# Convolution of large token groups in 32x32 tiles of the matmul array

## The chip, the cores and the metric

The kernel runs on one core of a Trainium2 chip. The metric is the time of one execution on the device in microseconds (us), taken as the median of several runs. A hardware profile of one execution gives the traces that are read here. The engines of the core are TensorE (PE, its weight loads are listed as PEld), VectorE (DVE), ScalarE (ACT), GpSimd (POOL) and SyncE (SP, which here only issues DMAs). SBUF is the on-chip memory of 128 partitions, PSUM the small memory that PE writes into, and DRAM the memory outside.

## The reference

The input x holds 8 sequences of 4160 tokens with 192 channels, in float32. The channels are 8 heads of 24. Two steps are computed.

```python
# step 1: causal convolution over 7 tokens, one softmaxed filter a head
w = softmax(weight)                                  # (8, 7)
y[b, s, h*24:(h+1)*24] = sum_k w[h, k] * x_pad[b, s + k, h*24:(h+1)*24]
# step 2: channel mix
xk = mu_k * y + (1 - mu_k) * y_prev                  # y_prev: the token before
xr = mu_r * y + (1 - mu_r) * y_prev
k  = maximum(xk @ w_k, 0)                            # 192 -> 1024
v  = (k * k) @ w_v                                   # 1024 -> 192
out = v / (1 + exp(-(xr @ w_r)))                     # w_r: 192 -> 192
```

The output is 8 x 4160 x 192 in float32. The kernel works in bf16 with sums in float32.

## The kernel before, in words

**Pairs, steps, slots, bundles.** The 8 sequences go in four pairs. Both sequences of a pair are worked on together: their transposed y, `yT`, has 128 partitions, 64 channels of the one and 64 of the other, in three chunks. A pair is cut into steps of 512 tokens (some are 256), 34 steps in all. A step is cut into slots; a slot is one PSUM tile of k, 128 hidden channels by 512 tokens by two sequences (`k_mm`, L537, then relu on ACT, `k_relu`, L549, then the square on DVE, `k_square`, L563). Four slots make a bundle, and there are 65 bundles. The order of all engines is written out by hand: `bundle_rest` (L861) emits a bundle's work, and tables (`early`, `mix_a`, `mix_b`, `mix_c`, `late`, `xt`, `rq`, `rs`, `vq`) say which piece of other work goes to which place of which bundle.

**What a bundle holds.** In order on PE: three blocks of k (18 matmuls of 512 columns), the gate product r (`r`, L594, 12 matmuls), the first half of v (`v_rows`, L625, 32 matmuls), the fourth block of k, the convolution units of this bundle if there are any, and the second half of v. `v_out` (L641) multiplies v by the gate on DVE and SP stores it. All PSUM tiles come from one ring of four tiles of two banks; a tile is reused when the engine that reads it is done. `diff` (L480), `scale` (L511) and `add_y` (L517) make xk and xr from `yT` on DVE; the `diff` of a step stands two bundles ahead of the step's first bundle, in `mix_c`.

**Convolution.** A filter over 7 tokens is a banded matrix `toe` over tokens, so the convolution is a matmul that contracts tokens. The tokens of a pair are cut into groups. The first four groups are small and are done in other ways at the start (`conv_t`, L371, which yields y transposed, with 128x32 tiles; `conv_mm`, L351). The other 14 groups, g4 to g17, are large: three of 10 and one of 8 for each of the last three pairs, with "10" meaning two halves of ten blocks of 56 tokens (1120 tokens). Block rows are 64 tokens of which 6 are the halo and 56 give results, so one matmul uses a 64x64 tile of the array. `conv_tiles` (L302) does one unit: two heads, 8 matmuls, two row tiles by two column tiles, one PSUM tile. `conv_tiles_out` (L319) casts it into the tile `y` on ACT, in one piece or in two where the heads straddle a chunk of 64 channels. A group has four units, two in each of two bundles that lie two apart.

**The way of a group.** For a group needed by the step whose first bundle is fb, the units stand in bundles fb - 9 and fb - 7. `x_tile` (L103) takes a tile from a pool of three, sets one element on DVE (L109), and `load_x` (L116) loads x with a cast to bf16 from POOL's queue (L136), 8 to 15 bundles before fb; the element on DVE holds the load back until DVE has come that far. After the last unit, `y_write` (L424) writes y to DRAM by four DMAs of SP's queue; two bundles later (one for the first two of these groups) `y_read` (L432) reads it back by one transposing DMA into `yT`. `y` has two tiles.

**Names that the prediction uses.** k_sb is relu's output, r_sb the gate, o_sb the output tile (three buffers), xb the x tile, ps_c, ps_k, ps_r, ps_v, ps_t the PSUM tiles of convolution, k, r, v and transposing convolution.

Of the kernel before, what the change touches and what calls it, by code (L numbers as in the profile page):

```python
# [7 lines left out]
FP32 = mybir.dt.float32  # L8
BF16 = mybir.dt.bfloat16
# [5 lines left out]
def kernel(  # L15
# [11 lines left out]
    nc = tc.nc  # L27

    B, S, D = x.shape
# [8 lines left out]
    BLK = 120  # L38
    GB = 10
    HB = 56  # L40
    NROW = -(-S // (2 * HB)) * 2 * HB
    BANK = 512
    STEP = 512
# [45 lines left out]
    for p in range(NPAIR):  # L89
        base = 0  # L90
        for nb, s, on_pe in (
            ((3, 0, True), (4, 1, True), (4, 2, True), (5, 3, True), (10, 4, False), (10, 6, False))
            if p == 0
            else ((10, 0, False), (10, 2, False), (10, 4, False), (8, 6, False))
        ):
            groups.append((p, base, nb, first_bundle[first_step[p] + s], on_pe))
            base += nb * (BLK if on_pe else 2 * HB)
        assert S <= base <= NROW


    xbs = {}

    def x_tile(g):  # L103
        p, base, nb, _, on_pe = groups[g]
        xb = three.tile([P, GB, 2, D], BF16, tag="xb", name="xb")
        xbs[g] = xb
        if g > 4:

            nc.vector.memset(xb[0:1, 0, 0, 0:2], 0.0)  # L109
        if base == 0:  # L110
            nc.gpsimd.memset(xb[0:32, 0, :, :], 0.0)  # L111
        if not on_pe and base + 2 * nb * HB > S:
            n0 = nb - (base + 2 * nb * HB - S) // HB - 1
            nc.gpsimd.memset(xb[Q:P, n0:nb, :, :], 0.0)

    def load_x(g):  # L116
        p, base, nb, _, on_pe = groups[g]
        xb = xbs[g]
        if on_pe:
            parts, step, rows = ((0, base),), BLK, P  # L120
        else:
            parts, step, rows = ((0, base), (Q, base + nb * HB)), HB, Q
        for s in range(2):
            b = 2 * p + s
            for q0, start in parts:
                lo, hi = 0, nb
                t0 = start - HALO
                if t0 < 0:
# [94 lines left out]
    def softmax():  # L223
        nc.vector.tensor_reduce(out=w_max, in_=w_raw, axis=mybir.AxisListType.X, op=ALU.max, negate=True)
        nc.scalar.activation(out=w_exp, in_=w_raw, func=AF.Exp, bias=w_max, accum_out=w_sum)
        nc.scalar.preload_act_table(AF.Sigmoid)
        xbs[0] = three.tile([P, GB, 2, D], BF16, tag="xb", name="xb")
        for c in range(NC):
            cs = slice(c * Q, (c + 1) * Q)
            nc.scalar.copy(out=xbs[0][:, : groups[0][2], :, cs], in_=x_f32[:, :, :, cs])  # L230
# [78 lines left out]

    def conv_tiles_out(g, c):  # L310

        m = groups[g][2] // 2
        ps = conv_ps.pop((g, c))
        y = ys[g]
        c0, c1 = 2 * c * G, 2 * (c + 1) * G
        cuts = [c0] + [a for a in range(Q, D, Q) if c0 < a < c1] + [c1]
        for a, b in zip(cuts, cuts[1:]):
            d = a // Q * 2 * Q + a % Q
            nc.scalar.copy(  # L319
                out=bass.AP(  # L320
                    tensor=y.tensor,
                    offset=y.offset + d,
                    ap=[y.ap[0], [m * 2 * D, 2], [2 * D, m], [Q, 2], [1, b - a]],
                ),
                in_=bass.AP(
                    tensor=ps.tensor,
                    offset=ps.offset + a - c0,
                    ap=[ps.ap[0], [BANK, 2], [4 * G, m], [2 * G, 2], [1, b - a]],
                ),
            )  # L330

    def conv_units(g):

# [76 lines left out]
    def new_yT(p):  # L410
        yTs[p] = two.tile([P, 3, -(-(YC + S) // 16) * 16], BF16, tag="yT", name="yT")
        y_drams[p] = dram.tile([NROW, 2 * D], BF16, tag=f"y{p % 2}", name="y_dram")
        nc.vector.memset(yTs[p][:, :, 0:YC], 0.0)


    def y_write(g):
        p, base, nb, _, _ = groups[g]
        if base == 0:
            new_yT(p)
        m = nb // 2  # L420
        for j in range(2):
            for i in range(2):
                r0 = base + (i * nb + j * m) * HB
                nc.sync.dma_start(  # L424
                    out=y_drams[p][r0 : r0 + m * HB, :].rearrange("(n t) c -> t n c", t=HB),
                    in_=ys[g][j * Q : j * Q + HB, i * m : (i + 1) * m, :],
                )

    def y_read(g):
        p, base, nb, _, _ = groups[g]  # L430
        r0, r1 = base, min(base + 2 * nb * HB, S)
        nc.sync.dma_start_transpose(  # L432
            out=yTs[p][:, :, YC + r0 : YC + r1], in_=y_drams[p][r0:r1, :]
        )
# [244 lines left out]
    def at(table, b, fn, *a):  # L679
        table.setdefault(b, []).append((fn, a))  # L680
# [7 lines left out]
    for g, (p, base, nb, fb, on_pe) in enumerate(groups):  # L688
        if g < 3:
            continue  # L690
        if p == 0:
            xs = {3: [1, 1], 4: [2, 2, 3, 3], 5: [4, 4, 5, 5]}[g]
        else:
            xs = [fb - 9] * 2 + [fb - 7] * 2
        for i, b in enumerate(xs):
            xt.setdefault(b, []).append((g, i))
        if not on_pe:
            at(late, xs[-1], y_write, g)

            at(mix_c if g == 4 else late, xs[-1] + (1 if g < 6 else 2), y_read, g)  # L700
        if g > 4:

# [53 lines left out]
    def prologue():  # L756
# [13 lines left out]
        nc.vector.memset(zeros, 0.0)  # L770
        nc.vector.memset(w_nrm, 0.0)
        nc.vector.memset(ones6, 1.0)
        x_tile(1)
        load_x(1)
        masks_tap()
# [85 lines left out]
    def bundle_rest(b, ns):  # L861
# [131 lines left out]
```

## Time and profile before

| what | value |
|---|---|
| median of the runs | 414.11 us (413.73 to 414.35, 3 runs) |
| span of the profiled execution | 412.2 us |
| lies around the span, by the median | 1.9 us |
| PE busy | 403.7 us |
| DVE busy | 370.5 us |
| ACT busy | 353.2 us |
| POOL busy | 64.1 us |
| matmuls of the large groups (L302) | 448, busy 16.6 us |
| casts of the large groups (L319) | 84, busy 50.7 us |

The span runs from the first to the last instruction in the profiled execution; that execution has no time of its own beside it, and the median of the runs stands for it. Busy is the time in which an engine works on at least one instruction. Matmuls overlap, so the busy time of a group of them is less than their number times the length of one. "The chain" is the work that ended last, followed back from the end: at each step to what released it. A row such as `204.98 1.88 ACT L319 CAST ... x3` gives start, length, engine, line, operation, shapes and how many were merged; brackets at its end give idle time before it and what ended that. SPq rows are DMA issues in SP's queue, their length is that of the issue and not of the transfer. In a table of windows a row gives the window, its length, the busy time of PE and of PEld with the number of instructions in it, the granted clock, the share of DMA time and GB/s.

### The profile page before, as it was taken

How to read it: one execution, taken by the hardware profiler on the slowest of the kernel's cores; microseconds unless marked ns; L12 is line 12 of the kernel's file. 1: busy time of each engine (PE TensorE's matmuls, PEld its weight loads, DVE VectorE, ACT ScalarE, POOL GpSimd, SP SyncE). 2: the span in 40 equal slices, each digit the busy share in tenths (PEclk: the TensorE clock that was granted, in tenths of full speed). 3: DMA queues.
4: the chain of work that ended last, by engine and by line, in shares of the span. 5: the costliest groups of instructions: out<-in, count | busy, mean ns of one | idle time of the engine just before them, and what ended most of it. 6: DMA issues, size and time to landing. Idle time of an engine off the chain costs nothing.

```text
span 412.2 us, 16799 instructions
## 1 busy us (share of the span) xinstructions
PE 403.7 (98%) x7349; PEld 301.7 (73%) x7350; DVE 370.5 (90%) x672; ACT 353.2 (86%) x426; POOL 64.1 (16%) x100
## 2 busy tenths in 40 slices
PE   7899999999999999999999999999999999999996
PEld 5567767767867777776777777777777777777795
DVE  5999799999999998999999999999989898999973
ACT  6899978889988888988888899888889888787781
POOL 8622023022040201104040110304000000000000
PEclk9999999999999999999999999999999999999999
DMA  9999989959978894998769697897863926321223
GB/s 141 192 200 194 191 200 190 253 133 194 198 110 211 151 214 118 200 218 113 198 121 229 156 196 182 111 226 130 188 163 100 184 82 175 107 67 53 80 80 115
DMA packets 137241, 65.58 MB, mean 159 GB/s; under 512 B 87356, under 2 KB 137168, under 8 KB 137168
## 3 DMA queue, kind: packets, MB, share of 16 engines
q1 hardware_dynamic: 95840, 48.42, 44.9%
q0 software_dynamic: 40528, 15.53, 33.0%
q8 instruction: 57, 0.93, 0.9%
q10 hardware_dynamic: 800, 0.57, 0.4%
q14 instruction: 16, 0.13, 0.1%
HBM read 31.62 MB, written 37.09 MB: 167 GB/s over the span
## 4 chain that ended last, share of the span: by engine, by line
PE 88%; DMA 4%; DVE 3%; ACT 2%; issue 1%; POOL 1%; SPq 0%; POOLq 0%
PE ps_v L625 39%; PE ps_k L537 37%; PE ps_r L594 7%; PE ps_c L302 3%; DMA yT<-y_dram 2%; DMA wk<-in_moe_w_k_dram 2%; DVE k L563 1%; PE ps_v L577 1%; DMA y_dram<-y 1%; ACT k_sb L549 1%; ACT y L319 0%; DVE d L480 0%; POOL xb L136 0%; DVE xr L511 0%; SPq L424 0%
## 5 line engine op out<-in xcount | busy, mean ns | idle before, releaser
L549 ACT ACTIVATE k_sb<-ps_k 128x1024 bf16<-128x1024 f32 x260 | 253.1, 1037 | 36.1 <-PE ps_k L537 35.2
L563 DVE TENSOR_TENSOR k<-k_sb 128x1024 bf16<-128x1024 bf16 x260 | 172.6, 685 | 28.3 <-ACT k_sb L549 27.9
L537 PE MATMUL ps_k<-xk,wk 64*128 64x512 bf16 (+1 forms) x1632 | 191.0, 367 | 1.2 <-DMA wk<-in_moe_w_k_dram 0.7
L625 PE MATMUL ps_v<-wv,k 64*128 64x192 bf16 x4032 | 188.2, 243 | 0.2 <-DVE k L563 0.2
L625 PEld LDWEIGHTS <-k 64*128 64x128 bf16 x4032 | 167.7, 94 | 13.6 <-issue 4.0
L537 PEld LDWEIGHTS <-wk 64*128 64x128 bf16 x1632 | 79.9, 94 | 59.6 <-DMA wk<-in_moe_w_k_dram 0.9
L136 POOL DMA_DIRECT2D xb<-in_x_dram x62 | 45.1, 738 | 171.2 <-issue 81.8
L641 DVE TENSOR_TENSOR o_sb<-ps_v,r_sb 128x768 f32<-128x768 f32 x64 | 60.8, 951 | 2.6 <-issue 2.4
L605 ACT ACTIVATE r_sb<-ps_r 128x768 bf16<-128x768 f32 x65 | 53.3, 821 | 10.6 <-PE ps_v L625 9.9
L319 ACT CAST y<-ps_c 128x960 bf16<-128x960 f32 (+5 forms) x84 | 50.7, 685 | 0.0
L594 PEld LDWEIGHTS <-xr 64*128 64x128 bf16 x780 | 34.5, 94 | 15.2 <-issue 1.0
L594 PE MATMUL ps_r<-wr,xr 64*128 64x192 bf16 x780 | 43.1, 243 | 0.5 <-DVE o_sb L641 0.5
L511 DVE TENSOR_SCALAR xr<-d,mu 128x512 bf16<-128x512 bf16 (+1 forms) x102 | 35.1, 348 | 0.0
L480 DVE TENSOR_TENSOR d<-yT 128x1536 bf16<-128x1536 bf16 (+4 forms) x36 | 31.3, 870 | 2.0 <-ACT yT L381 1.1
L511 DVE TENSOR_SCALAR xk<-d,mu 128x512 bf16<-128x512 bf16 (+1 forms) x99 | 32.0, 352 | 0.1
L517 DVE TENSOR_TENSOR xr<-xr,yT 128x1536 bf16<-128x1536 bf16 (+1 forms) x33 | 31.0, 938 | 1.1
L517 DVE TENSOR_TENSOR xk<-xk,yT 128x1536 bf16<-128x1536 bf16 (+3 forms) x33 | 30.4, 921 | 0.1
L302 PEld LDWEIGHTS <-toe 64*64 64x64 bf16 x448 | 9.6, 106 | 11.7 <-issue 10.7
L302 PE MATMUL ps_c<-xb,toe 64*64 64x240 bf16 (+1 forms) x448 | 16.6, 265 | 0.2 <-ACT k_sb L549 0.2
L464 POOL COPY y_tail<-yT 128x195 bf16<-128x195 bf16 x4 | 3.2, 796 | 64.9 <-DMA yT<-y_dram 64.8
L111 POOL MEMSET xb<- 32x384 bf16 x3 | 1.2, 407 | 45.2 <-DVE xb L109 39.2
L371 PEld LDWEIGHTS <-xb 128*32 128x32 bf16 (+3 forms) x264 | 5.3, 119 | 1.9 <-ACT xb L230 1.1
(57 smaller groups left out, 63.0 us busy)
## 6 DMA issues: line engine op xcount, KB each, us to landing
out_dram<-o_sb SPq DMA_DIRECT2D x128, 192.0 KB
xb<-in_x_dram POOLq DMA_DIRECT2D x40, 240.0 KB, 8.2
y_dram<-y SPq DMA_DIRECT2D x44, 210.0 KB
y_dram<-y SPq DMA_DIRECT2D x12, 168.0 KB
xb<-in_x_dram POOLq DMA_DIRECT2D x10, 192.0 KB, 5.5
xb<-in_x_dram POOLq DMA_DIRECT2D x6, 216.0 KB, 4.9
xb<-in_x_dram POOLq DMA_DIRECT2D x6, 144.0 KB, 5.3
wk<-in_moe_w_k_dram POOLq DMA_DIRECT2D x4, 192.0 KB, 7.1
```

Source lines behind the costliest of these rows:

```text
L136: nc.gpsimd.dma_start(out=xb[q0 : q0 + rows, lo:hi, s, :], in_=bass.AP(tensor=x.tensor, offset=x.offset + (b * S + t0 + lo * step) * D, ap ...
L302: nc.tensor.matmul(out=banks[j * Q : (j + 1) * Q, i, :, :, k * G : (k + 1) * G], lhsT=toe[q, h, q], rhs=xbs[g][q, j * m : (j + 1) * m, :, ...
L319: nc.scalar.copy(out=bass.AP(tensor=y.tensor, offset=y.offset + d, ap=[y.ap[0], [m * 2 * D, 2], [2 * D, m], [Q, 2], [1, b - a]],), in_=bas ...
L511: nc.vector.tensor_scalar(out=t[:, c, :L], in0=diffs[s][:, c, :L], scalar1=mu[:, i, c : c + 1], scalar2=None, op0=ALU.mult)
L517: nc.vector.tensor_tensor(out=o, in0=o, in1=y_of(s, sl, 0), op=ALU.add)
L537: nc.tensor.matmul(out=ps[:, i, f * L : (f + 1) * L], lhsT=wk[r, c, fs], rhs=xk[r, c, :L], start=c == 0 and f == 0, stop=c == NC - 1 and f ...
L549: nc.scalar.activation(out=k_sb, in_=ps.rearrange("p a b -> p (a b)"), func=AF.Relu)
L563: nc.vector.tensor_tensor(out=o, in0=i, in1=i, op=ALU.mult)
L594: nc.tensor.matmul(out=ps[:, i, k * D : (k + 1) * D], lhsT=xr[q, c, ts], rhs=wr[q, c, :], start=c == 0, stop=c == NC - 1,)
L605: nc.scalar.activation(out=r_sbs[s, j], in_=r_ps.pop((s, j))[:, :, 0 : 2 * D], func=AF.Sigmoid)
L625: nc.tensor.matmul(out=v_ps[s, j][:, bank, k * D : (k + 1) * D], lhsT=k2s[s][q, f, t * P : (t + 1) * P], rhs=wv[q, f, :], start=half == 0 ...
L641: nc.vector.tensor_tensor(out=o_sb.rearrange("p (b t) d -> p b (t d)", b=2), in0=v_ps.pop((s, j)), in1=r_sbs.pop((s, j)), op=ALU.mult,)
```

## The change

From the middle of the second pair on, groups have a third kind, marked `None` where `on_pe` was True or False: 80 blocks of 26 tokens, 2080 tokens a group. There are five of them, g8 to g12, in place of the ten groups g8 to g17 of before; g4 to g7 stay. The first, in the second pair, begins at token 2080 and overlaps the group before it, of which only the rows up to there are read back.

A block row is now 32 tokens, 6 of halo and 26 of results; four row tiles by four column tiles of 32x32 hold 16 matmuls. `conv_sparse` does one unit: two heads, 32 matmuls of 240 columns into two PSUM tiles, each row tile into a bank of its own. Then each of the two tiles is cast into its own `y` tile by the pieces of before. A group has four units, one in each of four bundles: fb - 11, -9, -7 and -5 (15, 16, 17 and 19 for the first one).

A group's `y` are both tiles of the pool. They are written by eight DMAs of 26 partitions by 10 blocks after the last unit, and read back in two halves, at the ends of bundles fb - 4 and fb - 1. The x tiles now come from two tiles of 20 blocks; the small groups 0 to 3 share one, 4 and 5 the next, 6 and 7 the next. A large group is loaded in two halves, one a sequence, 18 and 14 bundles ahead of fb (15 and 13 for the first), each held back by an element that DVE sets (`tie_x` for the second).

```diff
@@ groups
-            else ((10, 0, False), (10, 2, False), (10, 4, False), (8, 6, False))
+            else ((10, 0, False), (10, 2, False), (TG, 4, None))
+            if p == 1
+            else ((TG, 0, None), (TG, 4, None))
...
+            if on_pe is None:
+                base = min(base, S - nb * 4 * TB)
@@ x_tile
-        xb = three.tile([P, GB, 2, D], BF16, tag="xb", name="xb")
+        if g in (0, 4, 6) or g in sparse:
+            whole = two.tile([P, TG, 2, D], BF16, tag="xb", name="xb")
+            room[:] = [whole, 0]
+        xb = room[0][:, room[1] : room[1] + nb, :, :]
@@ load_x
+        elif g in sparse:
+            parts, step, rows = [(32 * i, base + i * nb * TB) for i in range(4)], TB, 32
...
-        for s in range(2):
+        for s in batches:
@@ new
+    def conv_sparse(g, c):
+        nb = groups[g][2]
+        m = nb // 4
+        if c == 0:
+            ys[g] = [two.tile([P, GB, 2 * D], BF16, tag="y", name="y") for _ in range(2)]
+        tiles = [ring.tile([P, 2, BANK], FP32, tag="k", name="ps_c") for _ in range(2)]
+        xb = xbs[g].rearrange("p (m j) s c -> p j m s c", j=4)
+        for k in range(2):
+            h = 2 * c + k
+            for i in range(4):
+                q = slice(32 * i, 32 * i + 32)
+                banks = tiles[i // 2][:, i % 2, 0 : m * 4 * G].rearrange("p (m s c) -> p m s c", m=m, s=2)
+                for j in range(4):
+                    nc.tensor.matmul(
+                        out=banks[32 * j : 32 * j + 32, :, :, k * G : (k + 1) * G],
+                        lhsT=toe[q, h, q],
+                        rhs=xb[q, j, :, :, h * G : (h + 1) * G],
+                        start=True,
+                        stop=True,
+                    )
+        for y, ps in zip(ys[g], tiles):
+            cast_tiles(y, ps, m, c)
@@ y_write
+        if g in sparse:
+            m = nb // 4
+            for half in range(2):
+                for j in range(4):
+                    nc.sync.dma_start(
+                        out=bass.AP(
+                            tensor=y_drams[p].tensor,
+                            offset=y_drams[p].offset + (base + (2 * half * nb + j) * TB) * 2 * D,
+                            ap=[[2 * D, TB], [4 * TB * 2 * D, 2 * m], [1, 2 * D]],
+                        ),
+                        in_=ys[g][half][32 * j : 32 * j + TB, :, :],
+                    )
+            return
@@ tables
+        elif p == 1:
+            xs = [fb - 9, fb - 8, fb - 7, fb - 5]
         else:
-            xs = [fb - 9] * 2 + [fb - 7] * 2
+            xs = [fb - 11, fb - 9, fb - 7, fb - 5]
...
+        if g in sparse:
+            at(late, fb - 4, y_read, g, slice(0, 1), 2)
+            at(late, fb - 1, y_read, g, slice(1, 2), 2)
+            b = fb - 18 if p > 1 else fb - 15
+            at(early, b, x_tile, g)
+            at(early, b, load_x, g, (0,))
+            b = fb - 14 if p > 1 else fb - 13
+            at(early, b, tie_x, g, 1)
+            at(early, b, load_x, g, (1,))
+            continue
@@ bundle_rest
         for u in units:
-            conv_tiles(*u)
-            conv_tiles_out(*u)
+            if u[0] in sparse:
+                conv_sparse(*u)
+            else:
+                conv_tiles(*u)
+                conv_tiles_out(*u)
```

TG is 20 and TB 26. `cast_tiles` is the body of the former `conv_tiles_out` with the tiles as arguments.

More of the change, by code (lines that the diff above doesn't have):

```diff
@@ L40 @@
     HB = 56
+    TB = 26
+    TG = 20
     NROW = -(-S // (2 * HB)) * 2 * HB
@@ L93, with tie_x @@
             if p == 0
-            else ((10, 0, False), (10, 2, False), (10, 4, False), (8, 6, False))
-        ):
+            else ((10, 0, False), (10, 2, False), (TG, 4, None))
+            if p == 1
+            else ((TG, 0, None), (TG, 4, None))
+        ):
+            if on_pe is None:
+                base = min(base, S - nb * 4 * TB)
             groups.append((p, base, nb, first_bundle[first_step[p] + s], on_pe))
-            base += nb * (BLK if on_pe else 2 * HB)
+            base += nb * (4 * TB if on_pe is None else BLK if on_pe else 2 * HB)
         assert S <= base <= NROW
-    xbs = {}
+    sparse = {g for g, grp in enumerate(groups) if grp[4] is None}
+    ends = [nxt[1] if nxt[0] == grp[0] else S for grp, nxt in zip(groups, groups[1:] + [(NPAIR,)])]
+    xbs, room = {}, []
+    def tie_x(g, s):
+        nc.vector.memset(xbs[g][0:1, 1, s, 0:2], 0.0)
     def x_tile(g):
         p, base, nb, _, on_pe = groups[g]
-        xb = three.tile([P, GB, 2, D], BF16, tag="xb", name="xb")
+        if g in (0, 4, 6) or g in sparse:
+            whole = two.tile([P, TG, 2, D], BF16, tag="xb", name="xb")
+            room[:] = [whole, 0]
+        xb = room[0][:, room[1] : room[1] + nb, :, :]
+        room[1] += nb
         xbs[g] = xb
@@ L109, in x_tile, with load_x @@
             nc.vector.memset(xb[0:1, 0, 0, 0:2], 0.0)
-        if base == 0:
+        if base == 0 and g > 0:
             nc.gpsimd.memset(xb[0:32, 0, :, :], 0.0)
-        if not on_pe and base + 2 * nb * HB > S:
+        if on_pe is False and base + 2 * nb * HB > S:
             n0 = nb - (base + 2 * nb * HB - S) // HB - 1
             nc.gpsimd.memset(xb[Q:P, n0:nb, :, :], 0.0)
-    def load_x(g):
+    def load_x(g, batches=range(2)):
         p, base, nb, _, on_pe = groups[g]
@@ L226, in softmax @@
         nc.scalar.preload_act_table(AF.Sigmoid)
-        xbs[0] = three.tile([P, GB, 2, D], BF16, tag="xb", name="xb")
         for c in range(NC):
             cs = slice(c * Q, (c + 1) * Q)
-            nc.scalar.copy(out=xbs[0][:, : groups[0][2], :, cs], in_=x_f32[:, :, :, cs])
+            nc.scalar.copy(out=xbs[0][:, :, :, cs], in_=x_f32[:, :, :, cs])
         nc.vector.reciprocal(out=w_sum, in_=w_sum)
@@ L310, in conv_tiles_out, with cast_tiles @@
     def conv_tiles_out(g, c):
-        m = groups[g][2] // 2
-        ps = conv_ps.pop((g, c))
-        y = ys[g]
+        cast_tiles(ys[g], conv_ps.pop((g, c)), groups[g][2] // 2, c)
+    def cast_tiles(y, ps, m, c):
         c0, c1 = 2 * c * G, 2 * (c + 1) * G
@@ L427, in y_write, with y_read @@
                 )
-    def y_read(g):
-        p, base, nb, _, _ = groups[g]
-        r0, r1 = base, min(base + 2 * nb * HB, S)
+    def y_read(g, part=slice(0, 1), of=1):
+        p, base = groups[g][:2]
+        n = (ends[g] - base) // of
+        r0, r1 = base + part.start * n, base + part.stop * n
         nc.sync.dma_start_transpose(
@@ L692 @@
             xs = {3: [1, 1], 4: [2, 2, 3, 3], 5: [4, 4, 5, 5]}[g]
+        elif g not in sparse:
+            xs = [fb - 9] * 2 + [fb - 7] * 2
+        elif p == 1:
+            xs = [fb - 9, fb - 8, fb - 7, fb - 5]
         else:
-            xs = [fb - 9] * 2 + [fb - 7] * 2
+            xs = [fb - 11, fb - 9, fb - 7, fb - 5]
         for i, b in enumerate(xs):
@@ L698 @@
             at(late, xs[-1], y_write, g)
+        if g in sparse:
[8 more added lines that the diff above has]
+            continue
+        if not on_pe:
             at(mix_c if g == 4 else late, xs[-1] + (1 if g < 6 else 2), y_read, g)
@@ L772, in prologue @@
         nc.vector.memset(ones6, 1.0)
+        x_tile(0)
         x_tile(1)
```

## The prediction

> **What bounds the kernel now.** I read the page first: the busy shares and the chain that ended last.
>
> ```profile
> span 412.2 us, 16799 instructions
> ...
> PE 403.7 (98%) x7349; PEld 301.7 (73%) x7350; DVE 370.5 (90%) x672; ACT 353.2 (86%) x426; POOL 64.1 (16%) x100
> ...
> PE 88%; DMA 4%; DVE 3%; ACT 2%; issue 1%; POOL 1%; SPq 0%; POOLq 0%
> ```
>
> TensorE (PE) carries 88% of the chain, so time taken from PE comes off the end, as long as ACT, at 86%, and DVE, at 90%, keep up. The share does not tell what one convolution costs. For that I read the chain in order of time over one bundle of the steady state:
>
> ```profile
> 199.61 1.94 PE ps_k L537 x18
> 201.55 0.51 PE ps_r L594 x12
> 202.06 1.32 PE ps_v L625 x32
> 203.38 0.65 PE ps_k L537 x6
> 204.03 0.53 PE ps_c L302 x16
> 204.56 1.43 PE ps_v L625 x32
> 205.99 1.94 PE ps_k L537 x18
> ```
>
> The columns are start, length, and what. The chain never leaves PE. A bundle without convolution is 1.94 + 0.49 + 1.32 + 0.65 + 1.32 = 5.72 us. One with it is 6.38: the convolution's 16 matmuls (two units of eight) show as 0.53, and the v matmuls behind them as 1.43 in place of 1.32, so such a slot costs 0.64. The short groups (8 blocks a half instead of 10, 192 columns a matmul instead of 240) show 0.45, so 0.56. Where ps_c stands alone, its 16 matmuls run 0.60 from the first start to the last end and one lasts 263 ns, so the starts spread over 0.34 (0.28 in short groups). The other 0.30 of the slot are its two edges, where the array goes from 64x128 tiles to smaller ones and back.
>
> **The change, part by part.**
>
> *Matmuls.* The ten groups from the middle of the second pair on fill 20 such slots, 14 long and 6 short: 14 x 0.64 + 6 x 0.56 = 12.3 us. After it five groups fill 20 slots too, one unit of 32 matmuls of 240 columns in each (640 in all, as the program's order shows). The trace has no 32x32 tile, so I bound its rate. Edges: 0.30, as now. Starts: two windows show how close different tiles start.
>
> ```profile
> 203.95:203.97 0.02, 0.01 (x4) 0.01 (x4) 1.00 0.14 48
> 17.78:17.80 0.01, 0.01 (x4) 0.01 (x4) 1.00 0.85 102
> ```
>
> The first is four 64x64 tiles of the convolution, the second four 128x32 tiles of the transposing convolution (L371): in 16 and 15 ns four weight loads and four matmuls have started. Their records lie 3.3 ns apart in L371, so 16 pairs need about 53 ns. The second row also says that four column tiles stream four different operands over all 128 partitions at once, which is as much as 16 tiles of 32x32 read. The second sixteen weight loads stand behind the first sixteen pairs; a load precedes its matmul by 100 ns (203.98 and 204.08 in the ps_c records). So 53 + 100 + 53, about 0.205 us from the first start to the last, and a slot of 0.505: 20 x 0.505 = 10.1, **2.2 us less**. Ends of this term: if the second sixteen start as soon as the first tile has streamed (106 ns, the usual distance of ps_c's rounds) the spread is 0.16 and the gain 3.1; at the pace of the 85 one-column matmuls (0.83 us busy less 0.17 for one, 7.9 ns a pair) it is 0.245 and the gain 1.4; if only two column tiles stream at a time, 0.34 and a loss of 0.5; if a pair takes 16 ns, the distance between the two row tiles of a ps_k pair, 0.50 and a loss of 3.7. I take 3.3 ns, since L371 and ps_c have the nearest shapes.
>
> A rule speaks against this. The Trainium skill, "TensorE: Matmul & The Clock Gate", section "Wait — 56ns, not 53.3ns?", says that starts of matmuls never come closer than some 25 ns. By that 32 of them would spread over 0.78 us, a slot would be 1.08 and the change lose 9.3 us. Its section "Measured speedup vs the span model" takes some 4 ns between different tiles. The rows above show 3 to 4 ns there, so I don't use the first rule.
>
> *Casts on ACT.* 60 casts before (42 of long groups, 18 of short) and 60 after, all of long form. A long group's two slots sum to 973 + 706 + 444 ns each, a short one's to 812 + 599 + 392: 40.5 us before, 42.5 after. ACT hides 2.0 us more, if its order allows it:
>
> ```profile
> 204.06 1.02 ACT L549 ACTIVATE k_sb<-ps_k 128x1024 bf16<-128x1024 f32 x1 [0.21 <-PE ps_k L537]
> 204.98 1.88 ACT L319 CAST y<-ps_c 128x960 bf16<-128x960 f32 x3
> 206.72 2.90 ACT L549 ACTIVATE k_sb<-ps_k 128x1024 bf16<-128x1024 f32 x3
> 209.86 0.81 ACT L605 ACTIVATE r_sb<-ps_r 128x768 bf16<-128x768 f32 x1 [0.23 <-PE ps_v L625]
> ```
>
> The casts start when the relu before them ends, not when the matmuls do, so they don't move. Now a slot has two casts (2 x 0.95 chained, 1.9) or four (2.30 less three overlaps of 0.12, 1.94): they end at 206.9, as now. The ring of four PSUM tiles gives the slot's second tile to the third k block of the next bundle, which starts at 207.1 (205.82 + 2 x 0.65). With slots 0.14 shorter it wants it at 206.97: covered, by some 0.05. The 0.23 of idle ACT before L605 is the other cover, of which 0.14 + 0.06 go. So the covers hold a gain of about 0.2 a slot, and no more. The first large group has units in three bundles in a row (15, 16, 17); stepping ACT through them leaves it 0.1 late once: **0.1 us**.
>
> *The trip through DRAM.* Eight writes of 26x10 rows of 768 B stand in SP's queue where four of 56x5 stood, and the group's first half is read one bundle after them instead of two. Behind the read's wait in SP's queue stand only output stores, with three buffers. SP and DVE:
>
> ```profile
> 36.07 3.06 SPq L424 DMA_DIRECT2D y_dram<-y  x4
> 39.23 1.62 SPq L649 DMA_DIRECT2D out_dram<-o_sb  x2
> 42.77 4.92 SPq L432 DMA_TRANSPOSE yT<-y_dram  x1
> ...
> 221.47 0.96 DVE L480 TENSOR_TENSOR d<-yT 128x1536 bf16<-128x1536 bf16 x1
> 222.34 0.69 DVE L563 TENSOR_TENSOR k<-k_sb 128x1024 bf16<-128x1024 bf16 x1
> 223.72 0.69 DVE L563 TENSOR_TENSOR k<-k_sb 128x1024 bf16<-128x1024 bf16 x1 [0.69 <-ACT k_sb L549]
> ```
>
> Take the bundle shown as a group's last: its first y tile is cast at 205.9, eight writes issue until 206.0 + 2 x 3.06 = 212.1, two stores (1.6 to 2.6 us) until 213.7 to 214.7, and then the read issues. It waits for the first four writes only; they land 6.55 after the first issue (36.07 to 42.62 in the chain), at 212.6. A read takes 6.88 from issue to landing on the chain, 2.0 more than its issue; the steady ones issue in 3.5, so 5.5 to 6.9, and up to 1.7 if the last writes are still in the queues (they land at 215.6). So yT is there between 219.2 and 223.3. The first diff on it is the one at 221.47, two slots earlier by 0.14: 221.2. Behind it DVE has 0.69 idle before a square that waits for ACT. The read is thus late past this cover by nothing to 1.4 us a group, five times, 0 to 7. Most of the interval lies ahead of 221.9, and I take **0.3 us** for all five.
>
> *The rest, at nothing.* Loads of x: half groups of 4 x 640 rows every four bundles on POOL where a group's 2560 rows stood, three to four bundles ahead of their use; POOL is busy 16%. Should a load be late, DVE's tie (59 ns) doesn't wait for it, only the slot would. The y tiles go back to ACT before the next casts, about 17.5 us after the last bundle's start, with their writes landed at 16. In the prologue group 4's load no longer waits for a buffer (0.6 us, hidden, its matmuls come 14 us later).
>
> Sum against the profiled execution: 412.2 - 2.2 + 0.1 + 0.3 = 410.4 of span. The runs' median 414.11 is 1.9 above that span, a part the change doesn't touch: **412.3 us**.
>
> **Rivals.**
>
> *The gain is swallowed by ACT.* If casts chain less well (2.12 in place of 1.88 a slot), the second tile comes free 0.2 later and the third k block takes back the 0.14: 20 x 0.14, and 414.0 us. For it: covers of 0.05. Against it: the casts' overlap is in the row above.
>
> *The read comes late.* The one on the slow side by a wait that did not exist. Price 1.0 a group (read at 6.9, with writes in the queue): 414.1 - 2.1 + 5.0 = 417.0. It decides from 0.4 a group; from 0.6 the kernel is slower by 0.2%. For it: the read issued at 42.77, with loads in flight, did hold up DVE (0.8 us) and behind it PE (ps_r 0.5, ps_k 0.3, by the view of waits). Against it: only one of fourteen did.
>
> *The tiles don't run side by side.* Break-even is a spread of 0.31 a slot, 10 ns a pair; at 16 ns 418, with two column tiles at a time 415. Then the change doesn't do what it says. Against it stands the L371 row.
>
> **How the numbers follow.** Forecast 0.60 (411.0 to 413.2, the gain term's near ends), swallowed 0.16, late read 0.14, tiles one after another 0.10. What can be told from no change is about 0.2%, 0.8 us: faster below 413.3, slower above 414.9. So 0.60, 0.16, 0.24. The low end is the gain of 3.1; the high end goes into the two slow cases, to 416.2, and leaves out the 16 ns and the late reads over 0.85 a group.
>
> **What would show it.** Right: ps_c in the later slots starts within 0.2 us and the bundle pair falls from 12.10 to about 11.96; no wait of PE on ACT's y; DVE's diffs without waits on the read. Wrong: ps_c over 0.5 us, ps_k waiting for y casts, or DVE d waiting for yT and PE ps_r for o_sb behind it.

## The result, and the profile after

The changed kernel takes 432.29 us (median of 4 runs, 429.30 to 441.58) where the kernel before takes 414.17 in the same comparison (413.73 to 414.35): 1.042 times as long, 95% interval 1.036 to 1.049. Runs over 1.5% above the fastest of their kernel count as slow and are left out of every ratio here: the one of 441.58 (mean granted clock 0.97) and two of experiment 1. The profiled execution took 429.41 us. The forecast of 412.3 was wrong in sign, and its range, up to 416.2, does not hold the time.

The page of the changed kernel, the span, the busy shares and the chain that ended last:

```profile
span 427.6 us, 17416 instructions
...
PE 404.8 (95%) x7670; PEld 303.7 (71%) x7670; DVE 370.5 (87%) x672; ACT 355.5 (83%) x426; POOL 57.7 (13%) x91
...
PE 61%; DMA 12%; DVE 11%; SPq 4%; ACT 3%; issue 3%; DVEq 0%; ACTq 0%
```

PE is busy for about as long as before (404.8 us against 403.7), but it carries 61% of the chain instead of 88%, and DMA carries 12% instead of 4%. So the new time is not work, it is waiting for a transfer. The chain in order of time over the end of the first large group (start, length, what) shows which:

```profile
133.51 0.35 PE ps_c L364 x32
133.87 1.43 PE ps_v L681 x32
...
145.06 10.68 DMA yT<-y_dram
...
155.76 0.96 DVE d L536
...
159.11 1.01 PE ps_r L650 x12
160.12 2.56 PE ps_v L681 x32
```

The first two lines are the change as it was meant. A unit of 32 matmuls shows as 0.35 where 16 matmuls showed as 0.53, and the v matmuls behind it still as 1.43. In 19 of the 20 slots the 32 matmuls take 0.162 to 0.164 us from the first start to the last (0.316 in the one of bundle 16), and the slot (0.35, and 0.11 more for v than its usual 1.32) takes 0.45. The third line is the loss: the first half of the group is read back for 10.68 us, and VectorE's difference d waits for it. The last line is an echo: v takes 2.56 instead of 1.32 because the granted clock fell to 0.50 after PE had stood still.

The view of waits tells how often (engine, what waits, for what: total us, times, longest):

```profile
DVE d L536 <- DMA yT<-y_dram: 16.7, 6, 4.9
PE ps_r L650 <- DVE o_sb L697: 13.6, 6, 4.2
```

Five of the six waits of d belong to the five large groups: 4.89, 4.03, 2.95, 2.06 and 1.86 us, 15.8 together. PE waits behind them, since the output product o_sb stands behind d on VectorE and PE's ps_r needs the PSUM tile that o_sb frees. SyncE's queue over the same stretch (start, length, what, count) shows how the read came to be late:

```profile
135.45 7.80 SPq L466 DMA_DIRECT2D y_dram<-y  x8
143.35 1.61 SPq L705 DMA_DIRECT2D out_dram<-o_sb  x2
145.06 4.50 SPq L488 DMA_TRANSPOSE yT<-y_dram  x1
```

Eight writes take 7.80 us to issue, the two stores behind them 1.61, and only then is the read issued, 9.6 us after the first write. It has landed 20.3 us after the first write; d wanted it 15.4 us after (at 150.87).

Taken by bundle (from the first relu of one to that of the next, in both traces), bundles 14 to 63 take 312.07 us where they took 298.99, so 13.1 more. Bundles 23, 31, 39, 47 and 55, where the five waits are, hold 6.09, 3.53, 2.76, 1.55 and 1.88 of it, 15.8. That this is also the sum of d's waits is chance: PE itself stood still for 13.1 us there (4.22, 3.31, 2.54, 1.33 and 1.71), and ps_r and v at the lowered clock add 1.75 in bundle 23 (1.01 for 0.50, 2.56 for 1.32). Two bundles in a row with one unit of the new kind in an old unit's place are together 0.10 to 0.24 shorter, about 3 in all. 15.8 less 3 is the 13.1, to 0.3 us.

### The profile page after: what moved, and what is told of

It is laid out like the page before. It is cut to its first block, busy times and chain, and to the rows that moved or that the text cites. A ratio compares the mean times of both kernels' runs of the same rounds, so it can differ in the third digit from the quotient of the medians.

```text
span 427.6 us, 17416 instructions
## 1 busy us (share of the span) xinstructions
PE 404.8 (95%) x7670; PEld 303.7 (71%) x7670; DVE 370.5 (87%) x672; ACT 355.5 (83%) x426; POOL 57.7 (13%) x91
## 4 chain that ended last, share of the span: by engine, by line
PE 61%; DMA 12%; DVE 11%; SPq 4%; ACT 3%; issue 3%; DVEq 0%; ACTq 0%
PE ps_v L681 27%; PE ps_k L593 25%; DMA yT<-y_dram 11%; PE ps_r L650 6%; DVE k L619 3%; DVE o_sb L697 3%; ACT k_sb L605 2%; DVE d L536 2%; DMA y_dram<-y 2%; SPq L705 2%; PE ps_v L633 1%; DVE xk L567 1%; SPq L488 1%; PE ps_c L364 1%; SPq L466 1%
## 5 line engine op out<-in xcount | busy, mean ns | idle before, releaser
L681 PEld LDWEIGHTS <-k 64*128 64x128 bf16 x4032 | 169.5, 94 | 13.1 <-issue 4.9
L593 PEld LDWEIGHTS <-wk 64*128 64x128 bf16 x1632 | 83.1, 94 | 57.5 <-issue 2.7
L154 POOL DMA_DIRECT2D xb<-in_x_dram x62 | 44.1, 720 | 180.2 <-DVE xb L113 102.8
L650 PE MATMUL ps_r<-wr,xr 64*128 64x192 bf16 x780 | 43.6, 244 | 13.6 <-DVE o_sb L697 13.6
L337 ACT CAST y<-ps_c 128x960 bf16<-128x960 f32 (+2 forms) x84 | 52.6, 707 | 0.0
L364 PEld LDWEIGHTS <-toe 32*32 32x32 bf16 x640 | 3.9, 87 | 8.3 <-issue 7.4
L364 PE MATMUL ps_c<-xb,toe 32*32 32x240 bf16 x640 | 8.6, 266 | 0.0
L413 PE MATMUL ps_t<-toe,xb 128*32 128x120 bf16 (+3 forms) x264 | 6.7, 272 | 0.8 <-ACT yT L423 0.5
```

The lines of the kernel that those rows point to most:

```text
L154: nc.gpsimd.dma_start(out=xb[q0 : q0 + rows, lo:hi, s, :], in_=bass.AP(tensor=x.tensor, offset=x.offset + (b * S + t0 + lo * step) * D, ap ...
L337: nc.scalar.copy(out=bass.AP(tensor=y.tensor, offset=y.offset + d, ap=[y.ap[0], [m * 2 * D, 2], [2 * D, m], [Q, 2], [1, b - a]],), in_=bas ...
L593: nc.tensor.matmul(out=ps[:, i, f * L : (f + 1) * L], lhsT=wk[r, c, fs], rhs=xk[r, c, :L], start=c == 0 and f == 0, stop=c == NC - 1 and f ...
L650: nc.tensor.matmul(out=ps[:, i, k * D : (k + 1) * D], lhsT=xr[q, c, ts], rhs=wr[q, c, :], start=c == 0, stop=c == NC - 1,)
L681: nc.tensor.matmul(out=v_ps[s, j][:, bank, k * D : (k + 1) * D], lhsT=k2s[s][q, f, t * P : (t + 1) * P], rhs=wv[q, f, :], start=half == 0 ...
```

## The experiments

The leading theory (A) was that the late first read of each large group is the whole loss and that the matmuls' 3.0 us are there behind it. Its rivals: (B) the larger x tiles, their loads or the fuller bundles cost time of their own; (C) the issue of eight writes and two stores is enough to be late, however short the read is. Later two theories of the eight writes stood against each other: (D) they are issued as fast as their bytes are carried away, and (E) SyncE needs its own time for each write. Line numbers in the experiments' profiles are a few higher than in the changed kernel where an edit adds lines above. Each experiment starts from the changed kernel unless it says otherwise.

**1. The reader comes later.** The difference of a large group's first step, and what hangs on it, stands one place later in VectorE's order.

```
+    late_fb = {groups[g][3] for g in sparse}
...
-            elif s == 4:
+            elif s == 4 or fb in late_fb:
                 at(mix_b, fb - 1, diff, s)
...
-            at(mix_b if s == 4 else mix_a, fb - 1, scale, s, 0, 0)
+            at(mix_b if s == 4 or fb in late_fb else mix_a, fb - 1, scale, s, 0, 0)
```

> Only the reader moves: the diff of the first step of each 2080-token group stands in mix_b of bundle fb - 1 instead of mix_c of fb - 2, some 4.3 us later. Theory A (the whole loss is VectorE waiting in order for the first half's read, 15.8 us in five waits, with PE behind it, and the clock that falls in the longest of them): the waits of d on yT fall from 4.9, 4.0, 3.0, 2.1, 1.9 us to at most 0.6, PE ps_r no longer waits for o_sb in the later part, the clock stays at 1.00, and the time is 411 to 413 us. Theory B (the 32x32 tiles, the casts or the new x tiles cost the time, and the waits only show it): the time stays above 420 us.

Measured: 421.11 us (416.89 to 425.75), ratio 1.009 (1.006 to 1.011) by the runs of 416.89 and 418.13; the latter was profiled. The waits of d in this kernel:

```profile
DVE d L536 <- DMA yT<-y_dram: 2.9, 3, 1.9
```

The five waits fall from 15.8 us to 2.6 (1.87 and 0.69; a third, of 0.4, is an early group's), and the profiled run is 11 us shorter. But the whole loss is not gone. Bundles 24, 32, 40 and 56 are 0.5 to 0.7 us longer than before, where those of the changed kernel are up to 0.2 shorter: in three of them PE's ps_r waits 0.30 to 0.48 us for o_sb, in bundle 40 v waits 0.59 with no releaser shown. (Bundle 16 is 0.8 longer, but 0.6 in the changed kernel already: it holds a unit where it had none.) So the late place saves 13 us of d's waiting and costs about 3 us of its own. This run alone leaves A and B both standing.

**2. The read goes ahead of the second half's writes.** In SyncE's queue the first read is issued behind four writes instead of eight.

```
             for half in range(2):
+                if half == 1:
+                    y_read(g, slice(0, 1), 2)
...
-            at(late, fb - 4, y_read, g, slice(0, 1), 2)
```

> Only the first half's read moves in SP's queue: it is issued between the first four and the second four writes instead of behind all eight and two output stores. Theory A: the read issues some 7 us earlier and lands some 7 to 10 us earlier, all five waits of d on yT vanish, and the time is 411 to 413 us. Theory B: above 420 us. A rival inside A, that the read takes 10 us wherever it stands because of its shape (1040 rows), would leave its length from issue to landing at 7 to 10.7 us, but still with no wait.

Measured: 452.81 us (447.55 to 453.51), ratio 1.090 (1.083 to 1.097), the slowest of all. The five waits of d are gone (the read of the first group is issued at 140.23 and has landed at 145.5). A worse one takes their place:

```profile
PE ps_r L652 <- ACT y L337: 30.1, 4, 8.7
```

The read waits for the landing of the four writes ahead of it, and the four writes behind it wait in SyncE's queue. They are the last readers of a y tile that ScalarE's casts want for the next group, two bundles on. ScalarE waits in front of the cast, its relus and sigmoids stand behind it, and PE waits for those. The miss teaches that the writes cannot wait either: the y tiles have two bundles of room, and the queue has one order.

**3. The x load that meets the read moves away.** The first half of a large group's x is loaded two bundles later. In the changed kernel this load starts 1.7 to 2.0 us behind the first read of the large group two before it, which happens in three of the five groups.

```
-            b = fb - 18 if p > 1 else fb - 15
+            b = fb - 16 if p > 1 else fb - 15
```

> Only the first half of the x load moves, from 18 to 16 bundles ahead of fb, so that it no longer starts while the first half's read of the group before is on its way. If the load's packets hold back the landing (the three reads with a load behind them landed 3.1 to 3.8 us after their last packet started, the two without 0.3 to 2.0), the first three waits of d fall by 2.5 to 3 us each to 2.4, 1.5 and 0.5, and the time by 8 to 10 us (clock included) to 419 to 421 us. If the load has no part in it, the waits stay and the time is that of the changed kernel, 429 to 435 us.

Measured: 420.50 us (419.43 to 421.82), ratio 1.016 (1.013 to 1.019).

```profile
DVE d L536 <- DMA yT<-y_dram: 9.4, 6, 2.7
```

The first two waits fall from 4.89 and 4.03 to 1.14 and 1.21, the third from 2.95 to 2.75 only, and the last two, whose read never met a load, stay at 2.16 and 1.83. In the changed kernel the three reads with a load starting behind them land 3.3 to 3.8 us after their last packet has started; here the same three land at most 2.0 after it. So a neighbouring load is worth up to 3.8 us of a read, but 1.1 to 2.8 us a group of lateness remain without any. The time is the expected one, the first three waits are not (2.4, 1.5 and 0.5 were expected).

**4. The read goes ahead of the two stores.**

```
-            at(late, fb - 4, y_read, g, slice(0, 1), 2)
+            at(late, fb - 5, y_read, g, slice(0, 1), 2)
```

> Only the two output stores change places with the first half's read in SP's queue: the read is issued right behind the eight writes, 1.8 us earlier. If the queue's order is one term of the lateness, each of the five waits of d falls by 1.0 to 1.8 us and the time by 5 to 9 us to 420 to 424 us. If what is ahead in the DMA rings decides (the second four writes' packets), the waits stay within 0.5 us and the time above 427 us.

Measured: 420.02 us (416.90 to 421.16), ratio 1.013 (1.009 to 1.018).

```profile
DVE d L536 <- DMA yT<-y_dram: 5.5, 3, 3.5
...
DVE o_sb L697 <- DMA out_dram<-o_sb: 1.8, 2, 1.4
```

At the first large group the read is issued 7.95 us after the first write instead of 9.6. Three of the five waits vanish, the first falls to 1.77 us, and the third grows from 2.95 to 3.51: its read lands 11.7 us after its issue. The stores, now behind the read, make o_sb wait for a free buffer, which it did not do in the large groups before.

**5. Plain reads.** The same bytes go into the same columns without the transposition, so the output is another, but every engine's work is in place.

```
-        nc.sync.dma_start_transpose(
-            out=yTs[p][:, :, YC + r0 : YC + r1], in_=y_drams[p][r0:r1, :]
-        )
+        n = r1 - r0
+        nc.sync.dma_start(
+            out=yTs[p][:, :, YC + r0 : YC + r1],
+            in_=bass.AP(
+                tensor=y_drams[p].tensor,
+                offset=y_drams[p].offset + r0 * 2 * D,
+                ap=[[3 * n, P], [n, 3], [1, n]],
+            ),
+        )
```

> The changed kernel with its reads of y made plain: the same bytes of y_dram go into the same columns of yT, in 2080-byte runs and without the transposition, so the output is not the reference's, but every instruction of the engines and every write, store and load is in its old place. Theory A (the loss of 15.8 us is the length and the late landing of the transposing read behind a late issue): a plain read of 0.8 MB is through in 5 us or less after its issue, against 8.7 to 10.7 us, the waits of d fall to 0 to 1 us each, and the time is 411 to 414 (the 3.0 us of the matmuls less up to 2 us of waits left). Rival B (the larger x tiles and their loads, the casts or the fuller bundles cost time of their own that the waits hide): the waits of d go and the time is still 415 or more. Rival C (the issue alone, 7.2 to 8.1 us of eight writes and two stores, is enough): the read is short and d still waits 2 us or more in three groups.

Measured: 419.54 us (418.14 to 424.30), ratio 1.015 (1.009 to 1.022). SyncE's queue at the first large group, and the waits:

```profile
132.80 7.96 SPq L466 DMA_DIRECT2D y_dram<-y  x8
140.86 1.37 SPq L711 DMA_DIRECT2D out_dram<-o_sb  x2
142.33 0.55 SPq L489 DMA_DIRECT2D yT<-y_dram  x1
```

```profile
DVE d L542 <- DMA yT<-y_dram: 12.3, 5, 4.5
```

The time falls by 10 to 13 us, but not to A's 411 to 414, and A's expectation that a plain read is through in 5 us is wrong. (The profiled run, of 424.30, is the longest of the four, so its waits are the large ones.) The read issued at 142.33 lands at 151.53, 9.2 us later, though nothing is transposed. d still waits 3.32, 4.49, 1.54, 2.10 and 0.89 us. The five plain reads land 7.2 to 10.4 us after their issue, the transposing ones 7.6 to 10.7. So in this profile the transposition is the smaller part of the trip, and the cause sits in front of the read and around it. In the medians it weighs more: 6.2 us of loss are left (against experiment 6). That three groups still wait 2 us or more is what C said, that the read is long is not. This gave theory D: between 136 and 146 us the windows of the changed kernel show 143 to 208 GB/s carried, and the eight writes with the two stores are 2.0 MB, which at 200 GB/s are 10 us. The first two writes of the first large group issue in 0.34 and 0.40 us, the others in 0.84 to 1.32.

**6. The kernel before with plain reads**, as a base for the rest (same edit, in the kernel before).

> The kernel before with its reads of y made plain in the same way (output not the reference's). Its reads land long before d needs them in every theory, so its time is that of the kernel before within 0.3 per cent: 413.3 to 415. If it is faster than 413 the transposing reads cost the kernel before something too (by their neighbours in the DMA engines), and the run of the changed kernel with plain reads has to be read against this one.

Measured: 413.33 us (412.93 to 414.47), ratio 0.999 (0.997 to 1.000), as expected.

**7. Half the bytes.** Plain reads, and each of the eight writes carries 192 of y's 384 columns, in as many runs.

```
-                            offset=y_drams[p].offset + (base + (2 * half * nb + j) * TB) * 2 * D,
-                            ap=[[2 * D, TB], [4 * TB * 2 * D, 2 * m], [1, 2 * D]],
+                            offset=y_drams[p].offset + base * 2 * D + (2 * half * nb + j) * TB * D,
+                            ap=[[D, TB], [4 * TB * D, 2 * m], [1, D]],
...
-                        in_=ys[g][half][32 * j : 32 * j + TB, :, :],
+                        in_=ys[g][half][32 * j : 32 * j + TB, :, 0:D],
```

> The changed kernel with plain reads, and each of the eight writes of a large group carries only the first 192 of y's 384 columns, packed (384-byte runs instead of 768; as many writes, as many runs, 0.78 MB instead of 1.56 MB; the read fetches as much as before, partly twice; the output is not the reference's). Theory D (the writes are issued as fast as the DMA engines carry them away, about 200 GB/s for 1.56 MB and two stores of 0.19 MB each, and the read stands behind them): the issue of the eight falls from 7.5 to 3 to 4 us, the read is issued 3.5 to 4.5 us earlier, the five waits of d (3.3, 4.5, 1.5, 2.1, 0.9 with plain reads) go but for 0.5 us in one or two, and the time is 410.5 to 413. Rival E (SyncE needs its time for each of the 260 runs of a write, whatever they carry): the issue stays 7 to 8 us, the waits stay, the time stays 418 or more.

Measured: 412.19 us (411.02 to 412.79), ratio 0.995 (0.993 to 0.997), half a per cent below the kernel before.

```profile
129.57 4.22 SPq L466 DMA_DIRECT2D y_dram<-y  x8
...
134.90 0.43 SPq L490 DMA_DIRECT2D yT<-y_dram  x1
```

Eight writes with as many runs issue in 3.8 to 4.9 us (7.3 to 8.0 with plain reads and all bytes), so SyncE's own time per write (E) is not what takes 7.8. The read is issued 5.3 us after the first write and has landed 11.3 after it, not 18.7. No wait of d on a read is left, and PE waits for nothing in the large groups. Bundles 14 to 63 take 296.63 us, 2.4 less than in the kernel before. That is most of the matmuls' 3.0 us; 0.2 of what is missing is the unit that moved from bundle 53 (0.57 shorter) to bundle 16 (0.80 longer). The x tiles, their loads and the casts are all in this kernel, so what B holds is a few tenths of a microsecond.

**8. The whole trip two bundles earlier**, with all bytes and plain reads. The first list of units is that of the first large group, the second that of the others, and the last line moves the second x load.

```
-            xs = [fb - 9, fb - 8, fb - 7, fb - 5]
+            xs = [fb - 9, fb - 8, fb - 7, fb - 6]
-            xs = [fb - 11, fb - 9, fb - 7, fb - 5]
+            xs = [fb - 13, fb - 11, fb - 9, fb - 7]
-            at(late, fb - 4, y_read, g, slice(0, 1), 2)
-            at(late, fb - 1, y_read, g, slice(1, 2), 2)
+            at(late, xs[-1] + 1, y_read, g, slice(0, 1), 2)
+            at(late, fb - 3, y_read, g, slice(1, 2), 2)
-            b = fb - 14 if p > 1 else fb - 13
+            b = fb - 16 if p > 1 else fb - 13
```

> The changed kernel with plain reads and the whole trip earlier: units, writes and first read of the large groups two bundles earlier (one bundle for the first of them), the second x load two bundles earlier. All bytes are moved. Theory A/D (only lateness costs): the five waits of d are gone; left are the matmuls' 3.0 us and the extra unit's 0.6 us, so the time is 410.5 to 412 against 413.3 of the kernel before with plain reads. Rival B (larger x tiles, loads, fuller bundles cost on their own): other waits of 0.4 us or more a group appear and the time is 413 or more.

Measured: 418.39 us (416.72 to 419.07), ratio 1.011 (1.008 to 1.014). The expectation of 410.5 to 412 was missed. The waits of d are gone in all five groups, but one other wait stands once:

```profile
PE ps_r L656 <- ACT y L337: 3.2, 1, 3.2
```

It is the wait of experiment 2 again, by this edit's own fault: the first large group's writes are issued at the end of bundle 18, and the second group's first casts want the y tiles in bundle 19. That bundle is 5.0 us longer.

**9. Half of the writes on GpSimd's queue**, plain reads.

```
-                    nc.sync.dma_start(
+                    (nc.gpsimd if half else nc.sync).dma_start(
```

> The changed kernel with plain reads, and the four writes of the second half of each large group issued on GpSimd's queue instead of SyncE's. Rival E (SyncE's own time for each write): the read is issued about 4 us earlier and lands 3.5 to 4 us earlier, the waits go but for 0.5 us. Theory D (the engines carry 200 to 250 GB/s whoever issues): the read is issued on SyncE 3 to 4 us earlier or waits for GpSimd's writes, but lands only 0.5 to 2 us earlier; the waits fall from 3.3, 4.5, 1.5, 2.1, 0.9 to about 2, 3, 0, 0.5, 0, and the time is 415 to 418.

Measured: 420.95 us (417.99 to 423.55), ratio 1.017 (1.010 to 1.023).

```profile
133.71 3.07 SPq L466 DMA_DIRECT2D y_dram<-y  x4
...
145.43 0.53 SPq L489 DMA_DIRECT2D yT<-y_dram  x1
```

SyncE has issued its four writes by 136.8 and two stores by 139.8, but the read waits for GpSimd's writes until 145.43, 11.7 us after the first write (9.5 with all on SyncE). It lands 1.25, 3.33, 0.76 and 0.69 us earlier after the first write than in experiment 5 in four groups, and 1.26 later in one. The last of the eight writes has landed 11.6 to 13.5 us after the first was issued, against 10.6 to 11.0 in experiment 5, so a second queue does not carry the bytes faster, as D says. The waits of d are 0.36, 0.41, 2.08, 0.73 and 0.22, less than D has them in the first two groups and more in the third. The time is above D's 415 to 418 in the median: the new waits of PE (on y casts, 1.1 us, and one of 1.4 with no releaser shown) were not foreseen.

**10. Two bundles earlier, with room for y.** Experiment 8 with the second large group's first unit in bundle 20.

```
-            xs = [fb - 13, fb - 11, fb - 9, fb - 7]
+            xs = [fb - 12 if g == 9 else fb - 13, fb - 11, fb - 9, fb - 7]
```

> The run with plain reads and the trip two bundles earlier, mended: the second large group's first unit stands one bundle later (bundle 20 instead of 19), so that the y tiles' writes of the first large group, issued at the end of bundle 18, have a bundle to be carried away before ScalarE casts into the tiles again. If the 5.0 us left in the run before stood there and nowhere else, no wait over 0.5 us is left in the large groups, and the time is 410 to 412, faster than the kernel before with plain reads (413.3) by the matmuls' 3.0 us less 0.6 to 0.8 for the extra unit in bundle 16. If it comes to 413 or more, something besides lateness costs.

Measured: 412.61 us (411.17 to 413.40), ratio 0.996 (0.995 to 0.998), 0.4% below the kernel before; 0.6 us above the expected interval in the median.

```profile
127.94 7.85 SPq L466 DMA_DIRECT2D y_dram<-y  x8
...
138.57 0.54 SPq L489 DMA_DIRECT2D yT<-y_dram  x1
```

The writes take their 7.85 us and the read lands 17.4 us after the first of them, as slow a trip as ever. But d does not wait for it, nor PE for any y cast: bundles 14 to 63 take 297.27 us, 1.7 less than in the kernel before. Against experiment 5 only the place of the units, of their trip and of one x load was moved, so with plain reads lateness was the loss. No run has this order with the transposing reads.

**11. The same bytes in the kernel before.** Experiment 6 with each of the four writes of a group issued a second time into a copy that nobody reads.

```
+                for to in (y_drams[p], copies[p]):
...
-                    out=y_drams[p][r0 : r0 + m * HB, :].rearrange("(n t) c -> t n c", t=HB),
+                        out=to[r0 : r0 + m * HB, :].rearrange("(n t) c -> t n c", t=HB),
```

> The kernel before with plain reads (output not the reference's), and each of a group's four writes is issued twice, the second time into a copy that nobody reads: eight writes of 1.68 MB as in the changed kernel, all matmuls, tiles and loads as before. Theory D (issue paced by the bytes): the issue goes from 2.4 to 3.0 us for four to 7 to 8.5 us for eight, not to twice 2.9; the reads, which land 1.7 to 2.7 us ahead of their d now, are issued 1 to 3 us later and land 2 to 4 us later among the copies, so that d waits 0.5 to 2 us in half of the ten groups and the time is 415 to 425. If the issue of eight is 6 us or less, the mis-sized issue came from something else in the changed kernel (its runs, its neighbours), and the time stays within 1 us of 413.3.

Measured: 418.61 us (416.62 to 419.65), ratio 1.012 (1.010 to 1.014). Groups of ten blocks issue their eight writes in 7.3 to 8.1 us (once 8.7), against 2.9 to 3.2 for four in experiment 6: 2.5 times, not twice. So the figure does not come from the writes of 26 rows; that it goes by the bytes is what experiment 7 shows. But d waits in one early group only (3.49 us at 52.44), not in half of ten as expected. In the later groups the read lands 14.6 to 18.1 us after the first write and nothing waits: a d at 187.91 goes ahead of the read that lands at 191.21, so the d that needs that read is the next, at 200.01, 26.7 us after the first write. The kernel before has that much distance where the changed one has 15.4. The median is 2 us above the profiled run; what the other runs waited for was not profiled.

## Why the prediction was wrong, point by point

**Matmuls: right, at the best end.** The forecast gave 20 slots of 0.505 and a gain of 2.2, with a low end of 0.16 for the spread and a gain of 3.1. Measured: spread 0.163, slot 0.45, so 20 slots in 9.0 us against 12.0 (14 of 0.627 and 6 of 0.546), a gain of 3.0. Within sixteen the starts lie 3.3 ns apart, as the L371 row said. The second sixteen start 113 ns after the first, and their weight loads stand 62 ns ahead of them, not 100 behind the first sixteen's 53; that was the part too long. Of the two rules of the Trainium skill weighed there ("TensorE: Matmul & The Clock Gate"), some 4 ns between tiles ("Measured speedup vs the span model") fits, since 0.163 us for 32 starts are 5 ns each; the 25 ns ("Wait — 56ns, not 53.3ns?") do not hold between different tiles.

**Casts: right.** L337 is busy 52.6 us against 50.7, and no wait of PE on a y cast shows in the changed kernel. The rival in which ACT swallows the gain did not happen; its 414.0 does not follow from its terms either (20 x 0.14 is 2.8, more than the whole gain of 2.2).

**The trip through DRAM: the step that failed.** It read "So yT is there between 219.2 and 223.3" and "I take **0.3 us** for all five". That is 13.2 to 17.3 us after the first write. The need was right: 15.2 by the working, 15.4 measured. The trip was mis-sized in two terms:
- "eight writes issue until 206.0 + 2 x 3.06 = 212.1": 6.1 for the eight, and 7.7 to 8.7 with the stores to the read's issue. Measured: 7.2 to 8.1, and 9.3 to 9.7. Doubling four writes was the error. In the first large group the first two writes go out in 0.34 and 0.40 us, the later ones take 0.84 to 1.32; experiment 7 shows that this pace follows the bytes, experiment 11 that four more writes take longer than the first four.
- "5.5 to 6.9, and up to 1.7 if the last writes are still in the queues". Measured from issue to landing: 10.68, 9.81, 9.28, 7.69 and 7.61; only the last two are inside. The writes are still under way at every one of these reads (the last lands 10.7 to 11.3 us after the first was issued), and the first three reads also meet the x load of the large group after the next. That load stood under "The rest, at nothing": it was looked at for its own due time only, and not for whom it meets.

All five landings, 17.3 to 20.3 us after the first write, lie at the late end of the interval or beyond it. Choosing a value near the early end ("Most of the interval lies ahead of 221.9") treated as an even spread terms that go up together: without the load the first read takes 6.1 us in place of 10.7 (experiment 3), and behind half the writes' bytes the plain reads, which fetch as much as before, take 5.2 to 6.1 in place of 7.2 to 10.4 (experiment 7). Which part of the way the writes, stores, read and load compete for is not shown: the DMA engines' mean share is 0.64 to 0.79 at the writes' 143 to 208 GB/s, and other windows of the same trace carry more.

**The rival "The read comes late"** had the right mechanism and its signs, DVE d waiting for yT and PE ps_r for o_sb behind it. Its price of 1.0 us a group was 1.9 to 4.9, and its chance of 0.14 too small. Its own evidence was misread: no load was in flight beside the read issued at 42.77, since x's last one had landed at 39.13, and the read took no longer than others. It held up DVE because d wanted it 12.8 us after the first write and it landed after 13.6. The later groups of that kernel have some 26.7 us (experiment 11); the change makes 15.4 the rule, with a longer trip.

**The sum.** Gain 3.0, the bundles with the waits 15.8 (the fall of the clock in the first of them was no term of the prediction), the rest of the span (0.55 at the start, 1.1 in bundles 0 to 13, 0.7 behind bundle 63) differs from run to run by about as much: the start is 0.85 earlier in experiment 5 and 0.85 later in experiment 1. Bundle 13 stays 0.5 to 0.8 longer in several runs with the transposing reads and not in those of experiments 5, 7 and 10; its cause is not settled.

## What to carry to other kernels

When a change makes a transfer's batch larger, take the bytes of all that is in flight in that stretch (writes, stores, the read itself and any load that starts beside it), divide by the rate the windows show, and set that against the distance from the first write to the reader. Here this estimate is a lower bound: 3.8 MB at 200 GB/s are 19 us for the first group, which took 20.3, and 2.8 MB without a load are 14 for the last two, which took 17.3 and 17.4. Do not scale the issue time of a shorter burst, whose first transfers go out before the pace of the bytes is felt. Where the distance falls short, move the whole trip earlier rather than reorder the queue: a transfer that goes first leaves another behind it, whose buffer is wanted too.

## What the runs showed of the hardware

- Sixteen 32x32 tiles of TensorE do work side by side: 32 matmuls of 240 columns on two rounds of sixteen tiles start within 0.162 to 0.164 us in 19 of 20 slots, and one lasts 0.27.
- The eight writes of a large group (1.6 MB in runs of 768 bytes, on one queue) had landed 10.7 to 11.3 us after the first was issued, and windows of 2.5 us in that stretch carried 143 to 208 GB/s. With half of them on a second queue the read behind them landed on the average 1 us earlier only. The Trainium skill, "DMA: Bandwidth & Descriptors", section "Measured (HBM→SBUF, 128 partitions, SWDGE, issued from GpSimd)", gives 341 GB/s for a load of 1 MB. That is the other direction, and no run here shows such a rate for these writes.
- In the changed kernel a transposing read with a load that starts 1.7 to 2.0 us behind it lands 3.3 to 3.8 us after its last packet has started (three reads), and the large groups' other reads 0.5 to 2.1 after it.
- The clock falls after some waits of PE and not after others: below are windows of the changed kernel behind the wait of 4.2 us.

```profile
160.20:161.20 1.00, 1.00 (x18) 1.00 (x15) 1.00 (x2) 0.77 (x1) 0.00 (x0) 0.50 1.15 327
161.20:162.20 1.00, 1.00 (x18) 1.00 (x14) 1.00 (x3) 0.00 (x0) 0.00 (x0) 0.50 1.47 203
```

The third number from the end is the granted clock: 0.50 for 3.4 us. After a wait of 3.3 us (at 212.02) and one of 3.2 (experiment 8) it stays at 1.00; after one of 2.7 in experiment 5 it falls all the same. The Trainium skill, "TensorE: Matmul & The Clock Gate", section "What's actually happening", has windows of 3.4 us that run on freely. The traces agree: each stretch between two changes of the clock is a whole multiple of 3.41 us (3.41, 10.24, 47.79 and 51.20 are among them). In windows laid off so from the first clock record of each of the 13 traces, the start and the end of the span left out, the clock fell behind all eight that had it at 1.00 and held 2.15 us or more without PE work, and behind none that held 1.94 or less. So the place of a wait decides with its length: the one of 3.3 us was cut by an edge into 1.77 and 1.54, the one of 2.7 had 2.15 in one window.
